# Two stores of the attention's output issued later, and a lag of two in the first two expert blocks

## The chip, the cores and the metric

The kernel runs on one core of a Trainium2 chip. The metric is the device time of one execution in microseconds; the time before is the median of three runs. Everything is computed in float32. The profile shows one further execution, with the engines TensorE (PE; its weight loads are listed apart as PEld), VectorE (DVE), ScalarE (ACT), GpSimd (POOL) and SyncE (SP), which here only issues DMAs. ACT and POOL issue DMAs too; a DMA that an engine issues stands in that engine's instruction queue.

## The reference

An RWKV-5 attention feeds a mixture of experts with one expert per token. Four sequences of 768 tokens, 8 heads of 48, so 384 features; 8 experts with a hidden layer of 1024.

```python
for t in range(S):
    kt, vt, rt = (k[:, :, t], v[:, :, t], r[:, :, t])
    cur = np.einsum('bhd,bhe->bhde', u[None] * kt, vt)
    y[:, :, t] = np.einsum('bhd,bhde->bhe', rt, state + cur)
    state = w[None, :, :, None] * state + np.einsum('bhd,bhe->bhde', kt, vt)
...
fresh_e = int(np.argmax(logits[b, s]))
if s == 0 or local_gate[b, s] < 0.5:
    e = fresh_e
else:
    e = prev_e if prev_e >= 0 else fresh_e
prev_e = e
...
h = np.maximum(x[b, s] @ w1[e], 0.0)
out[b, s] = p[e] * (h @ w2[e])
```

Here `x` is y with the heads of a token side by side, and `p` is the softmax of the token's logits.

## The kernel before

**Order.** The order of the instructions on every engine is written out by hand (`manual_schedule`): each engine runs its own in program order, and the framework adds the semaphore waits. A wait therefore holds up all that stands behind it on its engine. Tiles of a pool with few buffers are reused in turn; who writes a buffer again waits for the last readers of its old content, and a DMA that reads a tile is such a reader.

**Attention.** `Attention.run` goes through 16 items, four pairs of heads (`HP` is 4) of four sequences, one item in each step n. A step overlaps several items: loads three ahead (L194 rk, L198 kv, L199 vT, all issued by SP), products on POOL for item n + 1 (L216, L229, L212), scores (L288) and the item's own y (L267, L273) for the next items, `inside` and `before` for item n - 1, and `turn` for item n - 2. The last of them matter here:

- `before(n - 1)`: matmuls L310 finish the item's y in PSUM, and ACT's L318 copies it to the tile xT. There is one y accumulator in PSUM, so PE's L267 of the next item, the first to write it, waits for this copy.
- `turn(n - 2)`: PE transposes the item's two heads (L329) and ACT copies them in two instructions (L331) into the tile x of its sequence. x holds 768 tokens by 384 features; the pool has two buffers of it, so sequences 0 and 2 share one, 1 and 3 the other.
- After the sequence's last item, `turn` stores x to the DRAM tensor x_d (L334, 1152 KB in 768 rows of 1536 bytes, issued by ACT). Sequence 0 is stored in step 5, 1 in step 9, 2 in step 13, and 3 in the first expert block. The first items of sequences 2 and 3 are turned in steps 10 and 14.

The logits of a sequence are computed meanwhile, and the routing of the first two sequences runs on DVE, POOL and PE between the later items.

**Experts.** The tokens are gathered from x_d by their experts' lists (L1083, indirect DMAs on POOL). There are ten blocks (units). The first two (`EARLY` is 2) have 192 slots each and take tokens of the first two sequences only, so that PE has work while the routing of the other two is computed; the other eight, one for each expert, are larger and use products with fewer multiplications, spelled out elsewhere in `Experts.run`.

For the first two blocks, `hidden(i, m)` computes tile m (of eight) of the hidden layer: three matmuls of 128 x 192 (L1110, six entries in the trace), then the relu on ACT (L1113) into a tile hT, of which there are four buffers; its PSUM tile h has two. `output(i, m)` multiplies that tile by the second layer's weights and adds to three accumulators y (three matmuls, L1197, six entries). The loop over m puts `output(i, m - lag)` behind `hidden(i, m)`, with lag 1. What is left is put behind the loop; in the second block, which the first large block follows, the outputs of the last two tiles are handed to a list and placed between the matmuls of that block.

After the output of each m comes `routing(i * 8 + m)`, one step of the routing of the last two sequences: with transposes L709, L719 and L726, sums L746, L747, the choice of blocks and slots on DVE, and the matmuls L824 that sum token numbers (steps 7 and 12) and shares (steps 10 and 12). In step 8, after the first tile of the second block, L834 transposes the token lists. From it a chain on DVE (L843 to L855) makes the indices for the gathers of the third block, and goes on with `gates` (L906 to L911) and `weights` (L916, which writes val). The L824 of step 10 reads val. The transposes of gathered rows (L1096, copied by DVE's L1097) for the next block stand in the same loop, as do the sums of weights (L1145) and of tokens (L1134) of the first large block.

Of the kernel before, what the change touches and what calls it, by code (L numbers as in the profile page):

```python
# [20 lines left out]
P = 128  # L21
B, H, S, DH = 4, 8, 768, 48
HP = H // 2
# [4 lines left out]
DK, FK = D // P, F // P  # L28
# [33 lines left out]
class Attention:  # L62
# [260 lines left out]
    def turn(self, n, banks):  # L323

        nc, b, h0 = self.nc, self.items[n]["b"], 2 * self.items[n]["hp"]
        x = self.xs[b]
        for h in range(2):
            for c2 in range(C2):
                nc.tensor.transpose(banks[h][:, c2 * P:c2 * P + U], self.outputs(b, h0 + h)[:U, c2 * P:(c2 + 1) * P], self.ident[:U, :U])  # L329
        for h in range(2):  # L330
            nc.scalar.copy(x[:, :, (h0 + h) * DH:(h0 + h + 1) * DH],  # L331
                           banks[h][:, :C2 * P].rearrange("p (c e) -> p c e", e=DP)[..., :DH])
        if h0 == H - 2:
            nc.scalar.dma_start(out=self.x_d[b * S:(b + 1) * S, :].rearrange("(c p) d -> p c d", p=P), in_=x)  # L334

    def logits(self, b, bank):

# [14 lines left out]
    def run(self, router, fetch, heads):  # L352
# [11 lines left out]
        for n in range(M + 1):  # L364
# [69 lines left out]
            if n == g + 3:  # L434

                router.turn_runs(0, mp[:, mp_end:])
            self.before(n - 1)
            if M - 2 <= n < M:
                fetch(2 * (n - M + 2) + 1)
            if n == 6:  # L440
# [478 lines left out]
def route(tc, once, ps, lt, ident, gates):  # L919
# [57 lines left out]
    nc.vector.tensor_copy(ccol, cp[:NC, :1])  # L977
    run = tl("run", [NC, P])
    nc.vector.tensor_tensor_scan(run, rows, rows, ccol, Alu.max, Alu.max)
    rp = bank("rp")  # L980
    nc.tensor.transpose(rp[:, :NC], run, ident[:NC, :NC])
    ei = tl("ei", [P, NC], I32)
    nc.vector.tensor_copy(ei, rp[:, :NC])
# [15 lines left out]
class Experts:  # L999
# [49 lines left out]
    def fetch(self, i, engine):  # L1049
        u, wp = self.units[i], self.wps[i % 2]  # L1050
        if i < EARLY:
            w1, w2 = self.w1[u["e"]], self.w2[u["e"]]
        else:
            e = self.nc.values_load(self.router.order[0:1, i - EARLY:i - EARLY + 1], engines=[ET.SP], min_val=0, max_val=E - 1,
                                    skip_runtime_bounds_check_because="the blocks' experts are a permutation")
            w1, w2 = [w[bass.ds(e, 1)].rearrange("o p x -> (o p) x") for w in (self.w1, self.w2)]
        u["w1"] = wp.tile([P, FK, DK, P], F32, name="w1t", tag="w1t")
        engine.dma_start(out=u["w1"].rearrange("p m k f -> p (m k f)"), in_=w1)
        u["w2"] = wp.tile([P, FK, D], F32, name="w2t", tag="w2t")
        engine.dma_start(out=u["w2"].rearrange("p m f -> p (m f)"), in_=w2)  # L1060
# [349 lines left out]
    def run(self, att, flag, ready):  # L1410
        self.flag, self.spare, self.hs = flag, att.late, None
        n = len(self.units)
# [30 lines left out]
        def drained(i):  # L1443
            self.drain(i)
            sends.extend((i, j) for j in range(len(self.units[i]["rows"])))
# [5 lines left out]
        for i in range(n):  # L1451
# [60 lines left out]
                        self.send(*sends.pop(0))  # L1512
                continue

            lag = 4 if i == n - 1 else 1
            for m in range(FK):
                if following and m == FK - 1:
                    self.turn(i + 1, after - 1)
# [27 lines left out]
                    self.gather(i + 2, slice(j, j + 1), u[FK - 2 + j // 2])  # L1546

            if following:
                self.output(i, FK - 3)
                for step in self.token_sums(i + 1):  # L1550
                    step()
                self.both = False
                todo.extend(lambda i=i, m=m, d=d: self.output(i, m, (d,)) for m in range(FK - 2, FK) for d in range(DK))
                todo.append(lambda i=i: drained(i))
            elif i < n - 1:
                for m in range(FK - lag, FK):
                    self.output(i, m)
                drained(i)
# [193 lines left out]
```

## Time and profile before

| What | Time |
|---|---|
| median of the runs | 381.67 us |
| lowest and highest of the three runs | 381.08 and 381.85 us |
| the profiled execution's own time | 382.02 us |
| its span, first to last instruction | 380.2 us |
| attention, first load to the last item's y | 0 to about 109 us |
| first two expert blocks | 112.5 to about 150 us |
| granted PE clock, mean | 0.994 |

The page of the profile gives times in us from the span's start. A line of a timeline or of a group has the start or the count, the busy time, the engine, the line of the program, the operation, the tile written and the tiles read; in brackets stands how long the engine was idle before and what ended that. A q behind an engine's name marks its sequencer issuing a DMA. Matmuls are pipelined and their ends are modelled, so that PE's busy time also covers small gaps; starts are the better measure. In the slices a 9 means 90% busy or more. The DMA landings are read from semaphores; not every DMA's landing could be paired.

### The profile page before, as it was taken

The page shows a single profiled execution, that of the slowest core. Times are in us where ns is not written, and L with a number is a line of the kernel's source. Part 1 is how long each engine was busy: PE and PEld are TensorE (multiplying, and loading weights), DVE is VectorE, ACT ScalarE, POOL GpSimd, SP SyncE. Part 2 cuts the span into 40 slices and gives each one's busy share as a digit, 9 for nine tenths or more (in the row PEclk, how much of TensorE's full clock was granted, in tenths as well). Part 3 has the DMA queues.
Part 4 walks back from the last instruction along what each step waited for, and adds up shares of the span by engine and source line. Part 5 has one row for each costly group of instructions (what it writes and reads, how often), then busy time and mean ns, then how long its engine had stood idle before and what let it go on. Part 6 is the DMA issues. An engine that isn't in the chain of part 4 may idle for free. (4 is left out here: it accounts for less than half of the span.)

```text
span 380.2 us, 9697 instructions
## 1 busy us (share of the span) xinstructions
PE 366.5 (96%) x3846; PEld 323.6 (85%) x3846; DVE 249.2 (66%) x720; ACT 107.2 (28%) x295; POOL 151.2 (40%) x213
## 2 busy tenths in 40 slices
PE   8899999999999999999999999999999999999992
PEld 7676777776769989999999999999898899899971
DVE  6988778889853736587557857757658758466400
ACT  4132232232322112223323233233233233232210
POOL 7699999896222043211423213223323123012022
PEclk9999999999999999999999999999999999999997
DMA  7999999973738872811561254146146156063011
GB/s 255 413 411 407 409 395 338 378 276 128 246 121 288 331 275 72 320 53 39 202 219 42 68 222 174 35 174 228 56 167 232 34 181 228 12 225 161 3 37 36
DMA packets 17765, 74.97 MB, mean 197 GB/s; under 512 B 2761, under 2 KB 6618, under 8 KB 15408
## 3 DMA queue, kind: packets, MB, share of 16 engines
q1 hardware_dynamic: 10336, 56.89, 40.0%
q0 software_dynamic: 3424, 9.52, 7.5%
q10 hardware_dynamic: 3952, 7.87, 5.8%
q8 instruction: 32, 0.52, 0.6%
q14 instruction: 21, 0.17, 0.2%
HBM read 64.83 MB, written 9.51 MB: 196 GB/s over the span
## 5 line engine op out<-in xcount | busy, mean ns | idle before, releaser
L1309 POOL DMA_INDIRECT out_dram<-yo,sid x27 | 26.6, 986 | 102.2 <-ACT yo L1304 78.7
L1160 PE MATMUL h<-exT,w1t 128*128 128x168 f32 (+4 forms) x240 | 54.9, 327 | 0.0
L1164 DVE TENSOR_TENSOR hT<-h,hs 128x168 f32<-128x168 f32 (+3 forms) x60 | 21.1, 351 | 46.1 <-PE h L1160 30.5
L1083 POOL DMA_INDIRECT xg<-x_d,gid x29 | 31.2, 1076 | 36.2 <-DVE sm L906 17.4
L1160 PEld LDWEIGHTS h<-exT,w1t 128*128 128x128 f32 x240 | 41.6, 190 | 0.3 <-issue 0.3
L1110 PE MATMUL h<-exT,w1t 128*128 128x192 f32 (+1 forms) x192 | 38.3, 338 | 0.0
L1229 PE MATMUL y<-factors,sums 128*128 128x192 f32 x168 | 36.8, 326 | 0.0
L290 DVE TENSOR_TENSOR am<-pair,kept 128x768 f32<-128x768 f32 x32 | 29.9, 952 | 8.9 <-PE pair L288 8.7
L1160 PE MATMUL h<-xs,ws 128*128 128x168 f32 (+4 forms) x144 | 35.2, 326 | 0.0
L216 POOL TENSOR_TENSOR pd<-rk 128x384 f32<-128x384 f32 x32 | 31.4, 1003 | 7.7 <-PE y L267 5.5
L1110 PEld LDWEIGHTS h<-exT,w1t 128*128 128x128 f32 x192 | 32.3, 190 | 1.5 <-issue 0.2
L1160 PEld LDWEIGHTS h<-xs,ws 128*128 128x128 f32 x144 | 25.5, 190 | 4.3 <-ACT hs L1167 1.0
L1229 PEld LDWEIGHTS y<-factors,sums 128*128 128x128 f32 x168 | 28.9, 190 | 0.0
L212 POOL TENSOR_TENSOR ke<-kv,endT 128x288 f32<-128x288 f32 x32 | 24.9, 800 | 1.8 <-DMA kv<-in_kv_dram 1.8
L297 PE MATMUL y<-am,kv 128*64 128x128 f32 x360 | 22.8, 276 | 1.3 <-DVE y L273 1.2
L229 POOL TENSOR_TENSOR rw<-rk,tab 128x384 f32<-128x384 f32 x26 | 23.7, 936 | 0.2 <-DMA rk<-in_rk_dram 0.2
L288 PE MATMUL pair<-rw,kw 48*64 48x128 f32 (+1 forms) x768 | 23.0, 249 | 0.4
L1229 PE MATMUL y<-w2t,hT 128*128 128x192 f32 x96 | 23.0, 328 | 0.0
L1097 DVE COPY exT<-tp 128x384 f32<-128x384 f32 (+6 forms) x29 | 14.0, 489 | 13.6 <-PE tp L1096 13.4
L288 PEld LDWEIGHTS pair<-rw,kw 48*64 48x64 f32 x768 | 19.5, 133 | 2.6 <-POOL ke L212 0.6
L318 ACT COPY xT<-y 128x768 f32<-128x768 f32 x15 | 12.0, 799 | 33.6 <-PE y L310 33.6
L297 PEld LDWEIGHTS y<-am,kv 128*64 128x64 f32 x360 | 19.4, 137 | 2.4 <-DVE y L273 1.7
(301 smaller groups left out, 739.2 us busy)
## 6 DMA issues: line engine op xcount, KB each, us to landing
w1t<-in_w_dram SPq DMA_DIRECT2D x8, 1536.0 KB, 6.7
w2t<-in_w_dram SPq DMA_DIRECT2D x8, 1536.0 KB, 7.2
rk<-in_rk_dram SPq DMA_DIRECT2D x15, 768.0 KB, 9.1
kv<-in_kv_dram SPq DMA_DIRECT2D x16, 584.0 KB, 7.9
vT<-in_vT_dram SPq DMA_DIRECT2D x16, 384.0 KB, 10.0
x_d<-x ACTq DMA_DIRECT2D x4, 1152.0 KB, 9.5
w1t<-in_w_dram SPq DMA_DIRECT2D x2, 768.0 KB, 5.9
w2t<-in_w_dram SPq DMA_DIRECT2D x2, 768.0 KB, 5.4
```

The source lines that it names most:

```text
L212: nc.gpsimd.tensor_mul(t["ke"][:, p::2], t["k"][:, p::2], spread(self.endT[:, p, hp], 1, C2))
L216: nc.gpsimd.tensor_mul(t["pd"][:, z], t["rT"][:, z], t["kT"][:, z])
L229: engine.tensor_mul(t["rw"][:, z], t["rT"][:, z], spread(pw, 1, z.stop - z.start))
L288: nc.tensor.matmul(sc[f * DP:(f + 1) * DP, h, i, x:], lhsT=t["kw"][q, c, o * DP:(o + 1) * DP], rhs=t["rw"][q, c, x:], start=True, stop=True)
L290: return lambda: nc.vector.tensor_mul(t["am"][:, g], sc, spread(self.kept[:, g:g + 3], 1, 2))
L297: nc.tensor.matmul(t["y"][h][p * DP:(p + 1) * DP, c2 * P:(c2 + 1) * P], lhsT=t["v"][:, (2 * c + h) * DH:(2 * c + h) * DH + DP], rhs=t["am" ...
L1083: self.nc.gpsimd.indirect_dma_start(out=xg[:n], out_offset=None, in_=self.x_d[:rows], in_offset=bass.IndirectOffsetOnAxis(ap=u["gid"][:n, ...
L1110: nc.tensor.matmul(h[:, :n], lhsT=u["w1"][:, m, kk, :], rhs=u["xT"][:, kk, :], start=(kk == 0), stop=(kk == DK - 1))
L1160: nc.tensor.matmul(out, lhsT=a, rhs=b, start=start and k == 0, stop=stop and k == len(terms) - 1, skip_group_check=True)
L1164: nc.vector.tensor_tensor(out, a, b, op=Alu.add)
L1229: return lambda: nc.tensor.matmul(bank[:, x * half:(x + 1) * half], lhsT=a, rhs=b, start=(j == 0 and x == 0), stop=(j == FK // 2 - 1), ski ...
L1309: self.nc.gpsimd.indirect_dma_start(out=out.rearrange("n (h d) -> (n h) d", h=2) if half else out, out_offset=bass.IndirectOffsetOnAxis(ap ...
```

## The change

The store is taken out of `turn` for sequences 0 and 1 into a method of its own, which `run` calls in steps 8 and 12, behind `before`. In the blocks of the plain kind the lag is 2 where it was 1 (the last block keeps its 4), and behind the loop of the block before a large one the outputs of as many tiles as the lag leaves are put, up to tile 5.

```diff
@@ Attention.turn
-        if h0 == H - 2:
-            nc.scalar.dma_start(out=self.x_d[b * S:(b + 1) * S, :].rearrange("(c p) d -> p c d", p=P), in_=x)
+        if h0 == H - 2 and b >= 2:
+            self.store(b)
+
+    def store(self, b):
+        self.nc.scalar.dma_start(out=self.x_d[b * S:(b + 1) * S, :].rearrange("(c p) d -> p c d", p=P), in_=self.xs[b])
@@ Attention.run
             self.before(n - 1)
+            if n in (2 * HP, 3 * HP):
+                self.store(n // HP - 2)
             if M - 2 <= n < M:
@@ Experts.run
-            lag = 4 if i == n - 1 else 1
+            lag = 4 if i == n - 1 else 2
             for m in range(FK):
...
             if following:
-                self.output(i, FK - 3)
+                for m in range(FK - 2 - lag, FK - 2):
+                    self.output(i, m)
                 for step in self.token_sums(i + 1):
                     step()
```

## The prediction

> **What bounds the kernel now.** First the page's parts 1 and 2: busy time by engine, and the span in 40 slices of 9.5 us.
>
> ```profile
> span 380.2 us, 9697 instructions
> ...
> PE 366.5 (96%) x3846; PEld 323.6 (85%) x3846; DVE 249.2 (66%) x720; ACT 107.2 (28%) x295; POOL 151.2 (40%) x213
> ...
> PE   8899999999999999999999999999999999999992
> ...
> DMA  7999999973738872811561254146146156063011
> ```
>
> TensorE (PE) is busy 96% of the span, and in 10 us windows it is full from 150 to 370 us. So whatever PE gains or loses before 150 us is handed on to the end undiminished. Both edits lie before 150: the stores in the attention, the lag in the first two expert blocks. The chain of waits says only that the last scatter ends it; it is of no use here.
>
> Second, the timeline of ScalarE (ACT) where the first store is moved to (start, duration, line, and in brackets the idle time before):
>
> ```profile
> 59.73 0.80 ACT L318 COPY xT<-y 128x768 f32<-128x768 f32 x1 [2.09 <-PE y L310]
> ...
> 64.70 0.39 ACTq L334 DMA_DIRECT2D x_d<-x  x1
> ...
> 69.83 0.70 ACT L331 COPY x<-pair 128x288 f32<-128x288 f32 x2 [1.69 <-PE pair L329]
> 72.62 0.80 ACT L318 COPY xT<-y 128x768 f32<-128x768 f32 x1 [2.09 <-PE y L310]
> ```
> ```profile
> 73.47 0.88 PE L267 MATMUL y<-pd,w_t 48*64 48x384 f32 x8
> ```
>
> L318 empties PE's only y accumulator, and PE's next L267 starts 0.05 us after L318 ends (72.62 + 0.80 = 73.42, then 73.47; the same at 60.53 and 60.58). So L318 lies on PE's path with no slack. L331, in front of it in ACT's queue, ends at 70.53 and has 2.09 us of slack.
>
> Third, the tensor x_d, for how long a store takes to land:
>
> ```profile
> DMA to landing us min/median/max: 4.6/9.5/14.4
> ```
>
> The minimum is the store issued at 90.31, when no load runs; the maximum is that of sequence 0, issued at 40.35 among loads (landed at 54.78). For the store at 64.70 the landing isn't paired, but the trace's packet records end it at 76.9: 12.2 us.
>
> Fourth, the timeline in the second expert block, around the routing sums of L824:
>
> ```profile
> 132.55 0.27 PE L834 MATMUL tp<-ident,rows 128*128 128x128 f32 x1
> 132.66 1.14 PE L1110 MATMUL h<-exT,w1t 128*128 128x192 f32 x6
> 133.64 1.14 PE L1197 MATMUL y<-hT,w2t 128*128 128x192 f32 x6
> 134.62 1.14 PE L1110 MATMUL h<-exT,w1t 128*128 128x192 f32 x6
> 135.59 1.14 PE L1197 MATMUL y<-hT,w2t 128*128 128x192 f32 x6
> ```
> ```profile
> 135.94 1.02 DVE L916 TENSOR_TENSOR val<-eqv,pe 128x384 f32<-128x384 f32 x2
> ...
> 136.66 0.59 PEld L824 LDWEIGHTS mp<-ohq,val 128*32 128x32 f32 x24 [0.23 <-DVE val L916]
> ```
> ```profile
> 140.75 0.55 ACT L1113 ACTIVATE hT<-h 128x192 f32<-128x192 f32 x2 [4.57 <-PE h L1110]
> 141.14 0.95 PEld L1197 LDWEIGHTS y<-hT,w2t 128*128 128x128 f32 x6 [0.79 <-ACT hT L1113]
> 141.14 1.24 PE L1197 MATMUL y<-hT,w2t 128*128 128x192 f32 x6 [0.49 <-ACT hT L1113]
> ```
>
> A block of six matmuls starts 0.975 us after the one before. L824 needs val, the last of a VectorE (DVE) chain that starts from L834, and PE arrives there just as val is ready. The only PE idle time charged to lag 1 is the one at 141.14, where the relu L1113 was late.
>
> **The change, part by part.** No instruction is added or removed; four things move.
>
> *Store of sequence 0, from 40.35 to just after the L318 of step 8 (59.73 + 0.80 = 60.53).* Its issue takes 0.40 us of ACT, covered by the 2.73 us in which ACT idles until L343 at 63.26; uncovered it would cost 0.40. What it leaves: the loads of 44 to 55 run without it. I cost that at nothing: GpSimd (POOL) is back to back from 29 to 67 us, its last wait for a load is 0.68 us at 27.69, and PE waits for POOL, DVE and ACT there, not for loads. With that cover gone the most would be the store's own occupation, some 2.9 us (1.15 MB at 400 GB/s).
>
> What it adds: sequences 0 and 2 share one of two x buffers. The L331 at 69.83 is the first to write sequence 2 there, so it now waits for a store issued 9.3 us before it instead of 29.5. Behind it in ACT's queue stands L318, and PE's L267 waits for that. PE loses (landing + 0.06 for the wake + 0.70 for L331) - 72.62, that is landing - 71.86. Bounds: by the quiet store 60.53 + 4.64 = 65.2, nothing lost; by the slowest 60.53 + 14.43 = 74.96, 3.1 us lost. I take the store of 64.70, whose place among the loads is nearest (a rk load issued 1.4 us before it, here a kv load 1.6 us before): 60.53 + 12.2 = 72.7, 0.9 us lost. Nothing after it gives this back: the next PE idle time, 0.59 us at 80.88, ends on a DVE chain that PE itself feeds.
>
> [...]
>
> *Store of sequence 1, from 64.70 to after the L318 of step 12 (85.26).* The loads end at 85, so it is a quiet store: landed by 90, before its buffer's next writer at 94.96 and before the gather at 106.41. It passes L753 and L343 on ACT, with 2.17 us idle before L753. Nothing. SP's loads aren't reordered; each waits for the DMA eight earlier, and the kv load of 71.78 may now wait 1 us for the store, 11 us before POOL needs it.
>
> *Lag 2 in expert block 0.* One block L1197 of 0.975 us is deferred throughout, and both rests follow the loop. Every routing step comes 0.975 us earlier on PE and its DVE chain with it, so their distances stay. The gathered rows for the transpose at 127.01 (now about 126.0) landed at 125.55. Nothing.
>
> *Lag 2 in expert block 1.* All of block 0 is done before L834, so L834 stays at 132.55 and val's first half still comes at 136.49. Between L834 and L824 PE now has three blocks (L1110 twice, L1197 once) instead of four. It arrives 0.975 us earlier and waits that much: +0.97. Bounds: 0, if DVE were 0.97 faster (its thirteen operations run back to back from 132.86, so no), to 0.97. In return the wait at 141.14 goes: the relu of 140.75 is needed only after another L1110. Removed: 141.14 less 140.49, where the block would have started, 0.65; or nothing, if the late relu is an accident of the profiled execution. I take 0.65, as the row shows. Net +0.32. The two blocks L1197 after the loop give the differences of L1134 more time; no loss there.
>
> *Sum:* 0.9 + 0.3 = 1.2 us on the profiled execution (382.02 us, of which 1.8 lie around the span of 380.2): 383.2. The runs' median is 381.67, 0.35 below it; so I forecast 381.67 + 1.2 = **382.9**, with 382.4 to 384.0 as the case's own range.
>
> **The rivals.**
>
> *The store lands within the slack.* Eleven of the sixteen DMA engines had finished the store of 64.70 by 71.2, 6.5 us after issue; only stragglers took 12. If they are spared, landing is before 71.86 and only the expert part remains: 381.67 + 0.3 = 382.0, no change. For it: at 63.5 the loads are drained for 1.4 us. Against: both stores issued among loads had stragglers some 6 us behind.
>
> *Faster.* One mechanism: block L1197 no longer follows the relu by one block. For it: 0.65 at 141.14, and blocks that start about 0.1 late after a small transpose (119.51 instead of 119.41); five of these make 0.5. 381.67 - 1.15 = 380.5. It decides where val is ready before PE comes to L824 and the store lands in time. Against: these small gaps follow L719 and its like, not relus, and val has no slack.
>
> *Both waits in full.* Landing after 14.4 us (3.1), L824 waits 0.97, and the unprofiled runs had no late relu to save: 381.67 + 4.1 = 385.8. For it: the median is 0.35 below the profiled time. Against: the 14.4 came among three queued loads.
>
> *The change doesn't reorder what it says:* excluded; in the instruction orders of both programs the stores and the blocks stand as described, DVE's, POOL's and SP's unchanged.
>
> **How the numbers follow.** Main case 0.41, store in the slack 0.24, faster 0.17, both in full 0.18. About 0.2% (0.76 us) is what a measurement here can tell from no change: 380.9 to 382.4. Faster than that: 0.14, most of the third case. Within: 0.28, the second and the rest of the third and a little of the first. Slower: 0.58. The range 380.7 to 385.1 leaves out about half of the third case and half of the fourth.
>
> **What would show it.** Right: ACT's L331 of step 10 idle until a DMA x_d, then L318 and L267 late by landing less 71.86; PE idle about 1 us before the L824 near 136.7, released by val; no idle time of L1197 by the relu near 141. The 10 us windows after 150 stay full, shifted. Wrong: if L331 starts at 69.8 the store landed in time; if L824 waits for nothing, PE came there later than I think. A time below 380.9 would mean a gain that I did not see, most likely from the loads between 44 and 55.

## The result, and the profile after

| | before | after |
|---|---|---|
| median of 15 runs each | 381.94 us | 384.51 us |
| range of them | 381.08 to 383.77 us | 382.9 to 389.34 us |
| ratio, 95% interval | | 1.0064, 1.0046 to 1.0082 |
| profiled execution, its span | 382.02, 380.2 us | 385.74, 384.0 us |

The change makes the kernel slower by 0.64%, about 2.4 us. (The run of 389.34 us was disturbed and isn't in the ratio.) The time lies in the forecast's range (380.7 to 385.1), at twice the forecast step, and 0.5 us above the main case's own range (382.4 to 384.0). The profiled execution lost more, 3.8 us of span, and shows where. First the page's parts 1 and 2 after the change.

```profile
span 384.0 us, 9697 instructions
...
PE 366.9 (96%) x3846; PEld 324.4 (84%) x3846; DVE 249.1 (65%) x720; ACT 107.5 (28%) x295; POOL 151.6 (39%) x213
...
PE   7899999699989999999999999999999999999992
...
PEclk9999999989999999999999999999999999999998
DMA  7999988955765981730561155145246146064011
```

The number of instructions is the same. PE's row has a 6 in the eighth slice (67 to 77 us), and the row of the clock that PE was granted has an 8 in the ninth: two new things, side by side. (The 8 in PE's twelfth slice isn't one: PE's waits of 0.88 and 0.50 us at the end of the attention lay across two slices before, and lie in one now.) The same stretch in windows of 10 us, first before, then after; the columns after the window and its length are busy time (and instructions) of PE, PEld, DVE, ACT and POOL, the granted clock, the DMA engines' share and GB/s.

```profile
70.00:80.00 10.00, 10.00 (x248) 8.16 (x242) 9.31 (x18) 3.00 (x8) 9.73 (x12) 1.00 1.02 371
80.00:90.00 10.00, 9.41 (x181) 6.66 (x179) 9.04 (x13) 2.85 (x8) 9.12 (x10) 1.00 0.35 127
```
```profile
70.00:80.00 10.00, 7.14 (x137) 5.83 (x135) 7.02 (x12) 2.10 (x5) 7.10 (x9) 0.87 0.75 278
80.00:90.00 10.00, 10.00 (x237) 7.93 (x235) 7.33 (x13) 2.69 (x6) 7.61 (x9) 0.96 0.63 230
...
160.00:260.00 100.00, 100.00 (x628) 96.24 (x627) 68.46 (x237) 31.34 (x86) 25.37 (x33) 1.00 0.37 131
```

From 160 us on PE is full as before, only shifted. The loss is made between 70 and 90 us: PE has 2.86 us of idle time, and then a stretch at half its clock. Who ends the idle time is read from ACT's timeline and PE's (start, duration, engine, line; in brackets the idle time before and what ended it). The new line numbers are 3 to 5 higher than before from the store on.

```profile
59.17 0.80 ACT L318 COPY xT<-y 128x768 f32<-128x768 f32 x1 [2.09 <-PE y L310]
59.23 0.40 ACTq L337 DMA_DIRECT2D x_d<-x  x1
...
66.51 0.80 ACT L318 COPY xT<-y 128x768 f32<-128x768 f32 x1 [1.04 <-PE y L310]
74.61 0.70 ACT L331 COPY x<-pair 128x288 f32<-128x288 f32 x2 [7.31 <-DMA x_d<-x]
75.20 0.82 ACT L318 COPY xT<-y 128x768 f32<-128x768 f32 x1
...
82.37 0.80 ACT L318 COPY xT<-y 128x768 f32<-128x768 f32 x1 [0.67 <-PE y L310]
```
```profile
71.89 0.71 PE L288 MATMUL pair<-rw,kw 48*64 48x128 f32 x22
75.46 0.77 PE L288 MATMUL pair<-rw,kw 48*64 48x128 f32 x24 [2.86 <-ACT x L331]
```

The store of sequence 0 is issued at 59.23 and lands at 74.51. The tensor's own line has this as the longest landing of the four stores:

```profile
DMA to landing us min/median/max: 4.7/10.0/15.3
```

L331 of step 10 waits for that landing. PE waits for L331 one block of scores earlier than for L318: L331 empties the PSUM pair into which the second half of the scores goes. L318 of step 10 starts at 75.20 where it was 72.62, 2.58 later. L318 of step 11 is 4.16 later (82.37 against 78.21), that of step 12 3.56 (88.02 against 84.46), and the experts' first tile 3.66 (116.17 against 112.51). The lines, first before, then after:

```profile
78.21 0.80 ACT L318 COPY xT<-y 128x768 f32<-128x768 f32 x1 [0.67 <-PE y L310]
84.46 0.80 ACT L318 COPY xT<-y 128x768 f32<-128x768 f32 x1 [2.05 <-PE y L310]
112.51 1.23 PE L1110 MATMUL h<-exT,w1t 128*128 128x192 f32 x6
```
```profile
88.02 0.80 ACT L318 COPY xT<-y 128x768 f32<-128x768 f32 x1 [2.05 <-PE y L310]
116.17 1.23 PE L1115 MATMUL h<-exT,w1t 128*128 128x192 f32 x6
```

The trace's clock records give 0.5 from 77.30 to 80.71 us, 3.41 us long; before, the clock is 1.0 without a break from 7.34 us to 376 us.

In the second expert block, the timeline after the change:

```profile
139.61 1.02 DVE L921 TENSOR_TENSOR val<-eqv,pe 128x384 f32<-128x384 f32 x2
140.21 0.59 PEld L829 LDWEIGHTS mp<-ohq,val 128*32 128x32 f32 x24 [1.09 <-DVE val L921]
140.21 0.86 PE L829 MATMUL mp<-ohq,val 128*32 128x128 f32 x24 [0.79 <-DVE val L921]
...
143.74 0.33 ACT L1118 ACTIVATE hT<-h 128x192 f32<-128x192 f32 x1 [4.86 <-PE h L1115]
```

PE now waits 0.79 us for val, as forecast, and the relu L1118 is late once more but no PE instruction waits for it. The third block starts here, before and after:

```profile
149.82 0.54 PE L1160 MATMUL h<-exT,w1t 128*128 128x224 f32 x2
```
```profile
153.60 0.54 PE L1165 MATMUL h<-exT,w1t 128*128 128x224 f32 x2
```

From the experts' first tile to this line it took 37.31 us before (112.51 to 149.82) and takes 37.43 (116.17 to 153.60): 0.12 us more. So 3.66 of the 3.8 us come from the attention.

### The profile page after: what moved, and what is told of

Same layout as the page of the kernel before. It is cut to its first block, busy times and chain, and to the rows that moved or that the text cites. A ratio compares the mean times of both kernels' runs of the same rounds, so it can differ in the third digit from the quotient of the medians.

```text
span 384.0 us, 9697 instructions
## 1 busy us (share of the span) xinstructions
PE 366.9 (96%) x3846; PEld 324.4 (84%) x3846; DVE 249.1 (65%) x720; ACT 107.5 (28%) x295; POOL 151.6 (39%) x213
## 5 line engine op out<-in xcount | busy, mean ns | idle before, releaser
L297 PE MATMUL y<-am,kv 128*64 128x128 f32 x360 | 23.7, 282 | 1.3 <-DVE y L273 1.2
L297 PEld LDWEIGHTS y<-am,kv 128*64 128x64 f32 x360 | 20.2, 141 | 2.5 <-DVE y L273 1.7
L318 ACT COPY xT<-y 128x768 f32<-128x768 f32 x15 | 12.0, 802 | 31.3 <-PE y L310 31.3
## 6 DMA issues: line engine op xcount, KB each, us to landing
vT<-in_vT_dram SPq DMA_DIRECT2D x16, 384.0 KB, 4.7
```

Source lines behind the costliest of these rows:

```text
L297: nc.tensor.matmul(t["y"][h][p * DP:(p + 1) * DP, c2 * P:(c2 + 1) * P], lhsT=t["v"][:, (2 * c + h) * DH:(2 * c + h) * DH + DP], rhs=t["am" ...
```

## The experiments

Two questions: which part of the change costs, and what the clock has to do with it. Each kernel was timed beside runs of the kernel before on the same chip; ratios are against these.

**The stores alone.** The change with the lag as it was.

```diff
-            lag = 4 if i == n - 1 else 2
+            lag = 4 if i == n - 1 else 1
```

> Only the two stores are moved; the lag of the first two blocks is 1 as before. Theory: the store of sequence 0 lands some 15 us after its issue, L331 of step 10 waits for it, TensorE idles 2.9 us, and the clock then falls to one half for some 3.4 us; about 3.5 us of the 3.8 us by which the span grew come from here. So 2.3 to 2.6 us above the kernel before in the median (384.3 to 384.5), and a profile with L331 of step 10 waiting on x_d, a clock of 0.5 just behind it, and the first experts' matmul L1110 some 3.7 us later than before. Rival, that the lag costs most: not over 0.5 us above the kernel before (382.4).

384.58 us against 382.33, ratio 1.0063 (1.0043 to 1.0084): the whole loss. The line that shows the wait, on ACT:

```profile
73.63 0.70 ACT L331 COPY x<-pair 128x288 f32<-128x288 f32 x2 [6.52 <-DMA x_d<-x]
```

The clock is 0.5 from 74.21 to 81.04 us here, twice 3.41. The next lines show what that costs:

```profile
74.21 0.82 ACT L318 COPY xT<-y 128x768 f32<-128x768 f32 x1
82.75 0.80 ACT L318 COPY xT<-y 128x768 f32<-128x768 f32 x1 [0.67 <-PE y L310]
```
```profile
116.56 1.23 PE L1115 MATMUL h<-exT,w1t 128*128 128x192 f32 x6
```

L318 of step 10 is only 1.59 us later than before the change (PE was idle for 2.01 us), but that of step 11 is 4.54 later and the experts' first tile 4.05. In this execution more is lost behind the wait, while the clock is at half, than in the wait itself.

**The lag alone.** The kernel before with the changed lag and the two outputs behind the loop.

> Only the lag is 2; both stores stay where they were. Theory: the wait of the routing sums for val (0.8 us) against the wait for the late relu that goes (0.65 us): 0.1 to 0.3 us above the kernel before (382.0 to 382.3), with the wait for val in the profile and the attention's times unchanged. Rival, that the lag costs most of the change: 1.5 to 2.5 us above (383.5 to 384.4).

382.21 against 382.33, ratio 1.0009 (0.9992 to 1.0025): not to be told from no change. Its profile has the wait and no other PE idle time there:

```profile
136.34 0.86 PE L824 MATMUL mp<-ohq,val 128*32 128x128 f32 x24 [0.78 <-DVE val L916]
```

**The store of sequence 1 alone**, moved to step 12; the edit is shown against the kernel before, and the store is the method of the change.

```diff
-        if h0 == H - 2:
+        if h0 == H - 2 and b != 1:
...
+            if n == 3 * HP:
+                self.store(1)
```

> Only the store of sequence 1 is moved, to step 12; that of sequence 0 is where it was, the lag is 1. Theory, that this store costs nothing: within 0.5 us of the kernel before (381.5 to 382.8), no wait on x_d at L331, the clock at 1.0. Rival, that the loads between 65 and 77 us gain by its absence: 0.8 us or more under the kernel before. Other rival, that the late store holds up the gathers: 0.8 us or more above.

381.82 against 381.72, ratio 1.0001 (0.9986 to 1.0015). Nothing, either way.

**The store of sequence 0 one step earlier** (step 7 instead of 8), lag 1.

```diff
-            if n in (2 * HP, 3 * HP):
-                self.store(n // HP - 2)
+            if n in (2 * HP - 1, 3 * HP):
+                self.store(0 if n < 2 * HP else 1)
```

> Stores only (lag 1), that of sequence 0 one step earlier than in the change: issued near 54 us instead of 59. Theory, that only the landing after 71.8 us costs: it lands between 66 and 70 us even if it takes 12 to 15 us, L331 of step 10 waits for nothing or little, the clock stays at 1.0, and the time is that of the kernel before less the 0.4 us by which steps 4 to 8 are shorter: 381.4 to 382.0. Rival, that moving the store to the loads costs something at any place: 0.8 us or more above the kernel before (382.8 and up).

382.85 against 382.33, ratio 1.0017 (0.9998 to 1.0037). That is 0.5 us above the kernel before, between the two expectations; as an absolute figure it meets the rival's (382.8 and up). The store takes 13.80 us (54.35 to 68.15), hardly less than the others, but now lands before it is needed; the first write of sequence 2 waits for PE alone, and the clock stays at 1.0:

```profile
70.42 0.70 ACT L331 COPY x<-pair 128x288 f32<-128x288 f32 x2 [1.93 <-PE pair L329]
```

So most of the loss comes with a landing after about 71.9 us, and not with a late store as such. Whether the remaining 0.5 us is real isn't settled (the interval takes in 1); PE stands still 0.29 us at 62.39 inside L345, with no releaser named (see the last section).

**The wait taken away, the store left late.** Only the first pair of heads of sequence 2 is written before the store has landed. It goes to a small tile of its own here and is copied into x a step later; lag 1.

```diff
+            to = x[:, :, (h0 + h) * DH:(h0 + h + 1) * DH]
+            if (b, h0) == (2, 0):
+                if h == 0:
+                    self.side = self.late.tile([P, NCH, 2 * DH], F32, name="side", bufs=1)
+                to = self.side[:, :, h * DH:(h + 1) * DH]
+            nc.scalar.copy(to,
...
+            if n == 11:
+                self.nc.scalar.copy(self.xs[2][:, :, :2 * DH], self.side)
```

> Both stores late as in the change, lag 1, but the first write of sequence 2 (L331 of step 10) goes to a small tile of its own and is copied into x one step later, behind the L318 of step 11; so nothing in step 10 waits for the store of sequence 0. Theory, that this wait and the clock's fall after it are the whole loss: L331 of step 10 starts near 69.5 us, TensorE isn't idle there, the clock stays at 1.0, and the time is that of the kernel before less up to 0.4 us (381.4 to 382.2). Rival, that the store among the loads also makes TensorE's instructions late: in the traces so far its idle times without a releaser end 1.2 to 1.6 us after a 16 KB instruction packet has landed, and in the changed kernel such a packet lands at 73.5 us; then TensorE stands still near 73 us for 0.6 to 1.4 us with no releaser named, and the time is 0.5 to 1.3 us above the kernel before (382.3 to 383.2).

381.69 against 381.49, ratio 1.0003 (0.9992 to 1.0014). The store is as late as in the change (59.53 to 74.14), yet the loss is gone. On ACT and on PE:

```profile
69.54 0.70 ACT L336 COPY side<-pair 128x288 f32<-128x288 f32 x2 [1.92 <-PE pair L329]
```
```profile
73.18 0.53 PE L267 MATMUL y<-pd,w_t 48*64 48x384 f32 x1
74.48 0.87 PE L267 MATMUL y<-pd,w_t 48*64 48x384 f32 x7 [0.77 <-issue]
```

L331 (L336 here) starts where the theory has it, and the clock stays at 1.0. But the rival was right in its own point: PE stands still 0.77 us without a releaser in the middle of L267, though the time doesn't show it. So the loss of the change is the wait for the store and what follows from it; the gain of up to 0.4 us that the theory allowed a late store isn't seen in the time.

**The clock, first try.** The change with 18 small matmuls (36 entries in the trace) between the two halves of the scores of step 10, into columns that nothing reads.

```diff
+                if n == 10:
+                    for i in range(18):
+                        self.nc.tensor.matmul(mp[:, mp_end:], lhsT=self.ident, rhs=self.ident[:, :512 - mp_end], start=True, stop=True)
```

> The changed kernel with 18 small matmuls more in step 10 of the attention, in columns that nothing reads, queued where TensorE waits for L331: they take about 1 us or a little more of the 2.9 us of idle time. Theory, that the idle time makes the clock fall: with shorter gaps the clock stays at 1.0 behind the wait, the loss there is only the wait itself (2.6 us in the profile instead of 3.6), and the median is 0.5 to 1.2 us under the changed kernel (383.3 to 384.0). Rival, that the fall of the clock has another cause: the clock is 0.5 for 3.4 us all the same, and the time is that of the changed kernel or a little more (384.5 to 385.0).

391.37 against 382.33, ratio 1.0244 (1.0225 to 1.0263): much worse than either expected, and a miss of the experiment. PE's timeline:

```profile
73.67 6.45 PE L468 MATMUL mp<-ident 128*128 128x14 f32 x36 [0.76 <-DVE S L254]
80.04 1.33 PE L288 MATMUL pair<-rw,kw 48*64 48x128 f32 x24
```

The matmuls took 6.45 us instead of the expected 1, and the clock was 0.5 from 75.25 to 85.49 us, three times 3.41. In that stretch PE is busy by the profile, all 5.00 us of the window from 75 to 80. So here the clock didn't follow the time in which PE has an instruction, and filling with matmuls that move 14 columns didn't hold it up.

**The clock, second try**, with ordinary matmuls: the first half of the scores of step 10 issued four times.

```diff
-        for i in range(3):
+        for i in (0, 1, 2) * (4 if (n, g) == (11, 0) else 1):
```

> The changed kernel in which step 10 issues its first 24 score matmuls (L288, 0.71 us) four times instead of once, to the same place with the same operands: 2.13 us of ordinary matmuls more, queued just ahead of the wait for L331. The four traces so far show the clock changing on a grid of 3.413 us; it fell behind windows in which TensorE was busy for 0.54 and 0.49, and not behind windows of 0.60 and 0.62. Theory, that too little work in one such window makes it fall: the wait shrinks to some 0.7 us, no window before 85 us is under 0.7, the clock stays at 1.0, and the median is 0.4 to 1.1 us under the changed kernel (383.4 to 384.1), with L318 of step 10 still 2.6 us late and the first L1110 of the experts 2.6 us later than before instead of 3.7. Rival, that the fall has another cause, such as the transfers: the clock falls as in the changed kernel and the time is that of the changed kernel (384.5).

The store is as late as in the change (59.33 to 74.17) and L331 starts at 74.28, but the clock stays at 1.0. L318 of step 10 is at 74.86 and that of step 11 at 80.47, 2.24 and 2.26 us later than in the kernel before; the extra 1.58 us of the change between these two steps are gone. The experts' first tile comes 2.16 later (114.67) instead of 3.66. The lines, and the windows of this kernel:

```profile
74.86 0.82 ACT L318 COPY xT<-y 128x768 f32<-128x768 f32 x1
80.47 0.80 ACT L318 COPY xT<-y 128x768 f32<-128x768 f32 x1 [0.67 <-PE y L310]
114.67 1.23 PE L1115 MATMUL h<-exT,w1t 128*128 128x192 f32 x6
```

```profile
70.00:80.00 10.00, 8.73 (x236) 7.43 (x232) 7.15 (x12) 2.27 (x6) 7.12 (x9) 1.00 0.76 280
80.00:90.00 10.00, 9.51 (x228) 7.25 (x224) 8.52 (x15) 2.75 (x6) 8.79 (x11) 1.00 0.77 272
```

The median, 384.38 us (ratio 1.0058, 1.0035 to 1.0081), isn't lower than the change's, which the theory had wanted: the time is the rival's, while the profile is the theory's. The runs' mean clocks help to see why. In the change and in the stores alone, 11 of the 20 runs in the ratios have a mean clock of 0.992 or less and nine have 0.993 or more; the eleven took 384.25 to 387.55 us (median 385.62), the nine 382.9 to 384.04 (median 383.66). The two groups don't overlap. One stretch of 3.41 us at half clock takes 1.7 of 380 us from the mean, 0.0045; the runs of the kernel before that enter the ratios of the experiments all have 0.993 or more. All six runs with the repeated matmuls have 0.993 or more, and they took 383.67 to 384.8: the group of low clocks is gone. That the others pay for the repeats, most where the store lands early, would explain the median, but isn't shown. So by their mean clocks 11 of the 20 runs had the fall, and those are some 2 us slower. How much of the 2 us is the clock and how much a longer wait stays open. From L318 of step 10 to the experts' first tile the loss grew by 1.1 us in the profile of the change (2.58 to 3.66) and by 2.5 in that of the stores alone (1.59 to 4.05, clock at half for twice as long); with the repeats and no fall it didn't grow (2.24 to 2.16).

**The lag made to pay.** The kernel before with lag 2, and the routing sums of step 10 one routing step later, twice (on two chips).

```diff
-        if s == 10:
+        if s == 11:
             r.summed(0, 1)
```

> Lag 2 as in the change, both stores as before, and the second half's routing sums one routing step later, so that TensorE has a tile of both layers more to do before it comes to L824. Theory, that lag 2 trades the wait for the late relu (0.65 us) for the wait for val (0.8 us): here neither is left, and the time is 0.3 to 0.8 us under the kernel before (381.5 to 382.0). Rival, that the wait for the relu is hardly there without the profiler, or that the later sums hold up what follows: the time of the kernel with lag 2 alone or above (382.2 to 383).

> The kernel with lag 2, the stores as before and the routing sums a whole step later once more, beside other runs of the kernel before, since its first interval only touched 1. If the gain is real: 0.3 to 0.9 us under the kernel before again, with the interval under 1. If it was the scatter of the runs: within 0.2 us of the kernel before, as the one with the sums half a step later.

First 381.31 against 381.72, ratio 0.9982 (0.9965 to 1.0000); then 381.88 against 381.32, ratio 1.0007 (0.9994 to 1.0021). The first interval only touches 1, and the second run doesn't bear the gain out. In the first profile the waits for val and for the relu are both gone, and a new one has come, for the gathered rows of the next block:

```profile
142.56 0.55 PE L1096 MATMUL tp<-ident,xg 128*128 128x128 f32 x3 [1.32 <-DMA xg<-x_d,gid]
```

The second profile hasn't this wait, and its span is 379.6 us, but its runs show no gain. With the sums only half a step later:

> Lag 2, both stores as before, and the second half's routing sums L824 behind one more block of the first layer (half a step later instead of a whole step). Theory, that one block of 0.975 us covers the 0.8 us by which val is late, and that the gathered rows, which came 1.3 us late with the sums a whole step later, are now late by 0.4 us at most: 0.5 to 1.0 us under the kernel before (380.8 to 381.4). Rival, that the sums a whole step later were already all that this gives: as that kernel (381.3 to 381.7).

381.45 against 381.49, ratio 0.9997 (0.9985 to 1.0010), so half a step later gains nothing either. PE waits 0.94 us for the same gathered rows. In three of the five profiles with later sums (two of the five are of kernels further down) PE waits 0.8 to 1.3 us for gathered rows in place of val.

**Combinations.** The store of sequence 1 late, with lag 2 and the sums a step later:

> The two parts that should cost nothing together: the store of sequence 1 in step 12, lag 2, and the second half's sums one routing step later; the store of sequence 0 is where it was. Theory, that the parts simply add: 0.3 to 0.8 us under the kernel before (381.5 to 382.0), as the lag with the later sums alone. Rival, that the late store collides with the gathers and loads at the start of the experts: 0.5 us or more above that kernel.

381.32 against 381.72, ratio 0.9986 (0.9972 to 1.0000), the same as the lag part timed beside it, which did not hold up when it was run again. And the whole change with both waits taken away (the small tile, and the sums half a step later):

> The whole change with both waits taken away: stores late, lag 2, the first write of sequence 2 to a small tile of its own, and the sums half a step later. Theory, that the parts add: the time of the kernel with the small tile less 0.5 to 1.0 us, so 380.6 to 381.6 if that one is near the kernel before, and under both kernels. Rival, late instructions near 73 us: 0.5 us or more above the kernel with the later sums and the stores as before.

381.78 against 381.49, ratio 1.0021 (1.0008 to 1.0034). It undoes most of the loss of the change, but is a little slower than the kernel before. The theory that the parts add fell; from the small tile alone (1.0003) it can't be told for certain, since the intervals overlap. No version was found that beats the kernel before beyond the measurement's uncertainty.

## Why the prediction was right, and where its sizes were off

- *What bounds the kernel.* Right: what PE lost before 150 us came out at the end. 3.66 us at the experts' first tile plus 0.12 in the two blocks make the 3.8 us of the span.
- *Store of sequence 0, the wait.* The mechanism was right, and the step that failed is the size of its term: 0.9 us forecast, 2.58 measured at L318 of step 10. The working "landing less 71.86" gives 2.65 with the measured landing of 74.51, so the landing was wrong, not the formula. (Its 0.06 for the wake was an estimate; here L331 started 0.10 behind the landing, 74.61 against 74.51.) I took 12.2 us from the store at 64.70; it was 15.3 here, and 13.9 to 14.8 in the five other profiles with the store in step 8. The upper bound of 14.43 was also too low. I had put the issue behind the end of L318; it came 0.06 us after L318's start, which made the landing 1.3 us earlier than the working would have had it with 15.3. In the traces of before and after a store landed within 5 us only without loads beside it (4.64 at 90.31 before, 4.71 at 93.87 after).
- *"Nothing after it gives this back."* Two things followed that I had not counted. The clock fell to half for 3.41 us, and the loss was 4.16 us at step 11. And the next PE idle time, 0.59 us at 80.88, which I had called unable to give anything back, did so: it is gone in the profile after, and the loss at step 12 is 3.56. That the clock could fall wasn't among the terms, the rivals or the bounds.
- *Store of sequence 0, the loads relieved.* Costed at nothing, with a bound of 2.9 us from 400 GB/s; the page before has 395 to 413 GB/s in the slices from 9.5 to 57 us. L318 of step 8 came 0.56 us earlier (59.17 against 59.73). A gain was there in the steps up to 8. With the wait removed, it doesn't show in the time (ratio 1.0003).
- *Store of sequence 1.* Nothing forecast, ratio 1.0001 alone. Right.
- *Lag 2, block 0.* Nothing forecast; no new wait in that block.
- *Lag 2, block 1.* Forecast 0.97 lost to val and 0.65 regained from the relu, 0.32 net. Measured 0.79 lost, PE's idle time at the relu gone, 0.12 net in the profile; alone it is 1.0009, which can't be told from either. The mechanism was right.
- *The sum.* 1.2 us forecast. In the profiled execution the landing adds 1.7 (2.58 less 0.9) and the clock 1.0 (3.56 at step 12 less 2.58), and the lag takes 0.2 less than forecast: 3.7 of the 3.8 us. The runs' median lies lower, at 2.4 us. By their mean clocks, seven of the change's 14 runs in the ratio had a fall; their median is 3.7 us above that of the kernel before (385.62 against 381.94), that of the other seven 1.5 (383.42). As 1.5 is less than 2.58, the wait was probably shorter in those too, which no profile shows. That the time came to lie in the range is in part luck: the fall of the clock was in no sum, and the range had room for it only because it takes in part of the rival with both waits in full.
- *The rivals.* The store within the slack fell: no profile with the store in step 8 had it land before 73.2. (In the reading that spoke for it, the semaphore records have ten of the sixteen engines done with the store of 64.70 by 71.3, and the eleventh at 72.3.) Faster fell: the relu's wait isn't worth more than the waits that take its place, as the lag with later sums shows. Both waits in full, 385.8, is what the profiled execution came to (385.74), though not through the relu; for the median it was too much.

## What to carry to other kernels

Before a store is moved closer to the next writer of its buffer, take the longest landing seen under load as its price, and not the quiet one: here 15 us against 4.7. Even the longest seen before the change, 14.4, was too little. Waits of 2.01 and 2.86 us on TensorE cost a second time here, through its clock (0.5 for 6.83 and 3.41 us behind them); look at the granted clock behind every such idle time. Where a wait is removed by doing its work later, look for what stands next behind it: here the gathers, which took back 0.8 to 1.3 us.

## What the runs showed of the hardware

**The clock changed on a grid of 3.41 us, and it fell behind two windows that were about half busy, 1.66 and 1.84 us of 3.41.** All changes of the clock within a profile lie a multiple of 3.413 us after the first (in the change 77.30 lies 21 of them after 5.62, and 381.09 lies 110). Some windows cut along that grid, with PE's busy time in them and the clock behind them:

| Kernel | Window, us | PE busy, us of 3.41 | Clock behind it |
|---|---|---|---|
| stores alone | 70.80 to 74.21 | 1.66 | 0.5 |
| the change | 73.89 to 77.30 | 1.84 | 0.5 |
| small matmuls | 71.83 to 75.25 | 2.66 | 0.5 |
| the change | 70.47 to 73.89 | 2.13 | 1.0 |
| repeated scores | 73.24 to 76.65 | 2.49 | 1.0 |
| repeated scores, at the end of the kernel | 373.61 to 377.02 | 1.51 | 1.0 |
| the small tile, at the end | 371.46 to 374.88 | 1.56 | 1.0 |

So here no share of busy time alone decided. The two falls without added matmuls came behind the two emptiest windows of all profiles between 10 and 360 us, with 1.66 and 1.84 us of work; the next emptiest have 2.03 us (the kernel before at 102.9 us is one), and no fall behind them. But at the end of two kernels windows of 1.51 and 1.56 us had none either, and with the small matmuls one of 2.66 us had. The matmuls differ: in the attention's two windows nearly all have 48 rows or 48 columns, at the end they are 128 x 64. Whether that is the reason isn't shown. Nor is it shown whether it matters where on the grid a gap lies: no run moved one along it. At the ends of the kernels the clock fell behind windows with little or no work: in the change at 381.09, behind 0.00 us of work from 377.68 on, and in the kernel before at 375.98, behind 0.29 us from 372.57 on. The two falls of the attention came behind more work than that.

**TensorE's idle times without a releaser ended 1.2 to 1.5 us after packets of instructions had landed.** The packet records have a queue of 16 KB instruction packets, 32 in the change. In the profiles of all kernels run, PE has 15 idle times of over 0.25 us between 45 and 85 us for which no releaser is named; each ended 1.2 to 1.5 us after such a packet had landed. In this stretch a packet landed every 4.6 to 7.1 us in the kernel before and in the change; most have no such idle time behind them, and the kernel before has none. Seven of them:

| Kernel | PE idle, us | packet landed | PE on after |
|---|---|---|---|
| the change | 67.41 to 67.78 | 66.49 | 1.28 us |
| stores alone | 67.21 to 67.64 | 66.44 | 1.20 us |
| store in step 7 | 62.39 to 62.68 | 61.21 | 1.46 us |
| repeated scores | 72.89 to 74.16 | 72.93 | 1.22 us |
| the small tile | 73.71 to 74.48 | 73.10 | 1.37 us |
| store of sequence 1 late | 51.13 to 51.82 | 50.41 | 1.41 us |
| the same, lag 2, sums a step later | 79.51 to 80.82 | 79.35 | 1.47 us |

Whether the packets cause these idle times isn't shown: no run moved them alone.
